# Gated linear attention in pairs of chunks: two chunks' products side by side, the state known two chunks ahead, and a start of its own

## The chip, the cores and the metric

The kernel runs on one core of one Trainium2 chip. A core has TensorE (matmuls and transposes), VectorE, ScalarE and GpSimd for elementwise work, and queues from which DMAs are issued; SyncE, ScalarE and GpSimd issue them here. The metric is the device time of one execution in microseconds (us), the median of several runs. The profile is that of one execution; its span (432.3 us) is a little shorter than the time of the run it was taken in (434.06 us).

## The reference, cut to what matters

Two stages follow one another. The first is a gated recurrence over 768 steps for 4 x 8 heads of 48 features; the second sends each of the 3072 resulting tokens through the one of 8 experts that its gate likes best.

```python
def _attn_ref(q, k, v, alpha):              # each (4, 8, 768, 48)
    for t in range(S):
        state = alpha[:, :, t, :, None] * state + einsum('bhd,bhe->bhde', k[:, :, t], v[:, :, t])
        y[:, :, t] = einsum('bhd,bhde->bhe', q[:, :, t], state)

def _moe_ref(x, w_gate, w1, w2):            # x (3072, 384), 8 experts, hidden 1024
    expert_idx = argmax(x @ w_gate, axis=1)
    # rows sorted by expert; for each expert e:
    #   y = relu(x_e @ w1[e]) @ w2[e]
    return gate_w[:, None] * y              # gate_w: softmax weight of the chosen expert
```

The kernel cuts each sequence into 6 chunks of 128 steps, 24 chunks in all (`s` = 0 to 23; `c = s % 6` is the place in the sequence). Within a chunk the recurrence is a masked product of matrices; between chunks only a state `U` of 48 x 48 per head is carried.

## The kernel before: the parts that the change touches

For one chunk the work is, by name: `logs` (ln of alpha), `cums` (running sum of the logs by a triangular matmul, then the two exponentials), `decay_out` and `decay_in` (the chunk's total decay goes through DRAM to be turned from a row into columns `E`), `operands` (k and q times the exponentials), `transposes`, `scores` (k times q, masked), `attend` (results from the state, from the scores, and the products for the next state), `rows` (back to tokens x features, with the gate logits), `keep_rows` (to DRAM). Every four chunks `choose` picks the experts, `rank_products` and `slots_of` count the ranks, `one_hots` prepare the table from which `tokens_of_slots` builds the gather lists.

```python
def transposes(s):
    for i, n in enumerate(("kT", "qT")):
        tp = ps.tile([C, NP, C], F32, name="tp", bufs=2)
        for p in range(NP):
            nc.tensor.transpose(tp[:, p, :], pair(kqb[s % 4][:, i], p), ident[:])
        ...                                  # qT copied by VectorE, kT by ScalarE

def scores(s):                               # 48-row operands, 128-column outputs
    for p in range(NP):
        for t, r in ((sA, 0), (sB, DP)):
            nc.tensor.matmul(t[:, p, :], lhsT=d["kT"][r : r + D, p, :], rhs=d["qT"][r : r + D, p, :], ...)
    # dA = sA * cmask on VectorE; dB = copy of sB on ScalarE, masked by GpSimd

def attend(s):
    ...
    if c > 0:                                # from the state: 48 rows, 64 columns
        for n in range(NP // 2):
            for p in (n, n + NP // 2):
                for a in range(2):
                    nc.tensor.matmul(yp(p)[...], lhsT=st[s - 1]["U"][r : r + D, p, :], rhs=d["qT"][r : r + D, p, :], ...)
    for p in range(NP):                      # from the scores: 128 rows, 64 columns
        for a in range(2):
            nc.tensor.matmul(yp(p)[...], lhsT=d["v"][:, 2 * p + a, :], rhs=d["d" + "AB"[a]][:, p, :], ...)
    if c + 1 < NB:                           # for the next state: 128 rows, 64 columns
        ... nc.tensor.matmul(kv[...], lhsT=kqb[s % 4][:, 0, 2 * p + i, :], rhs=d["v"][:, 2 * p + i, :D], ...)
    nc.vector.tensor_copy(d["yT"][:, : NP // 2, :], y[:])
    nc.vector.tensor_copy(d["yT"][:, NP // 2 :, :], y2)
    # U = (kv + U of s-1) * E : VectorE adds, GpSimd multiplies

for s in range(-4, NT - 1):                  # one chunk per turn
    loads(s + 5)
    do(attend, s)
    do(scores, s + 1)
    ...                                      # ranks, when a group of chunks is complete
    do(cums, s + 3)
    do(operands, s + 3)
    ...                                      # one_hots or slots_of
    do(transposes, s + 2)
    do(rows, s)
    do(keep_rows, s)
    do(decay_out, s + 3)
    do(decay_in, s + 2)
    do(logs, s + 4)
    late_consts(s)
    ...                                      # choose; some loads of expert 0's weights

s = NT - 1                                   # the end of the stage
attend(s)
...                                          # transposes of two blocks gathered early
while hots:
    one_hots(hots.pop(0))
tokens_of_slots(0, 9)
slots_of(*rank_products(groups_of[-2], ...)) # chunks 21 and 22
rows(s); keep_rows(s); choose(groups_of[-1]) # chunk 23
one_hots(hots.pop(0), nc.gpsimd); one_hots(hots.pop(0))
tokens_of_slots(9, NT - 3)
go_ahead(1)                                  # steps of expert 0's first layer on the early blocks
slots_of(*rank_products(groups_of[-1], ...))
go_ahead(4)
one_hots(hots.pop(0))
tokens_of_slots(NT - 3, NT)
slots(0); fetch_lot(1, ...)                  # the other gathers of expert 0
```

Every engine takes its instructions in the order in which this program names them. After the attention stage the experts follow, from about 160 us to the end; the change does not touch them.

Of the kernel before, what the change touches and what calls it, by code (L numbers as in the profile page):

```python
# [8 lines left out]
F32 = mybir.dt.float32  # L9
# [9 lines left out]
def kernel(  # L19
# [10 lines left out]
):  # L30

# [54 lines left out]
    ends = list(range(0, NT - 7, 4)) + [NT - 5, NT - 3, NT - 1, NT]  # L86
    groups_of = [range(a, b) for a, b in zip(ends, ends[1:])]
    ORD = NT - 5

    TE = ORD - ORD % 4  # L90
    EB = 2
    EC = EB * C
    assert EB * C <= TE * C < N and TE * C > N // 2 and EB * NQ <= NU
# [189 lines left out]
    with tc.tile_pool(name="ld", bufs=6) as ld, \  # L283
# [20 lines left out]
        def loads(s):  # L304
            load("k", s + 1)
            load("q", s + 1)
            load("a", s + 2)
            load("v", s)
# [11 lines left out]
        def cums(s):  # L320
            d = st[s]
            cum = rps.tile([C, Dm], F32, name="cum")
            nc.tensor.matmul(cum[:], lhsT=cmask[:], rhs=d["ln"][:], start=True, stop=True)  # L323
            d["icp"] = work.tile([C, Dm], F32, name="icp")
            d["cp"] = work.tile([C, Dm], F32, name="cp", bufs=3)
            nc.scalar.activation(d["icp"][:], cum[:], AF.Exp, scale=-1.0)  # L326
            nc.scalar.activation(d["cp"][:], cum[:], AF.Exp)
# [15 lines left out]
        def operands(s):  # L343
            d = st[s]
            kq = kqb[s % 4]
            nc.gpsimd.tensor_tensor(kq[:, 0, :, :D], d["k"][:], heads(d["icp"]), op=ALU.mult)  # L346
            nc.gpsimd.tensor_tensor(kq[:, 1, :, :D], d["q"][:], heads(d["cp"]), op=ALU.mult)  # L347

        def transposes(s):
            d = st[s]  # L350
            for i, n in enumerate(("kT", "qT")):
# [3 lines left out]
                d[n] = work.tile([C, NP, C], F32, name=n, bufs=3)  # L355
# [23 lines left out]
        def attend(s):  # L379

            d = st[s]
            c = s % NB

            y = ps.tile([C, NP // 2, C], F32, name="y")
            kvp = ps.tile([C, 2 * C + NP * D + 4 * E], F32, name="kvp")
            y2 = kvp[:, : 2 * C].rearrange("r (p t) -> r p t", p=NP // 2)
            kv = kvp[:, 2 * C : 2 * C + NP * D].rearrange("r (p d) -> r p d", p=NP)

            def yp(p):
                return y[:, p, :] if p < NP // 2 else y2[:, p - NP // 2, :]  # L390

            if c > 0:
                for n in range(NP // 2):
                    for p in (n, n + NP // 2):
                        for a in range(2):
                            r = a * DP
                            nc.tensor.matmul(  # L397
                                yp(p)[at(p, a) : at(p, a) + DP, :],
                                lhsT=st[s - 1]["U"][r : r + D, p, :], rhs=d["qT"][r : r + D, p, :],
                                start=(n == 0), stop=False, skip_group_check=True,  # L400
                            )
            for p in range(NP):
                for a in range(2):
                    nc.tensor.matmul(  # L404
                        yp(p)[at(p, a) : at(p, a) + DP, :], lhsT=d["v"][:, 2 * p + a, :], rhs=d["d" + "AB"[a]][:, p, :],
                        start=(c == 0 and p % (NP // 2) == 0), stop=True, skip_group_check=True,
                    )
            d["yT"] = work.tile([C, NP, C], F32, name="yT")
            d["ranks"] = kvp[:, 2 * C + NP * D :]
            if c + 1 < NB:  # L410
                for p in range(NP):
                    for i, r in enumerate((0, DP)):
                        nc.tensor.matmul(  # L413
                            kv[r : r + DP, p, :], lhsT=kqb[s % 4][:, 0, 2 * p + i, :], rhs=d["v"][:, 2 * p + i, :D],
                            start=False, stop=True, skip_group_check=True,
                        )
            nc.vector.tensor_copy(d["yT"][:, : NP // 2, :], y[:])
            nc.vector.tensor_copy(d["yT"][:, NP // 2 :, :], y2)
            if c + 1 < NB:
                d["U"] = Ub[s % len(Ub)]  # L420
                E_b = d["E"][:].unsqueeze(2).to_broadcast([C, NP, D])
                if c > 0:
                    acc = work.tile([C, NP, D], F32, name="acc")
                    nc.vector.tensor_tensor(acc[:], kv[:], st[s - 1]["U"][:, :, :D], op=ALU.add)
                    nc.gpsimd.tensor_tensor(d["U"][:, :, :D], acc[:], E_b, op=ALU.mult)
                else:
                    nc.vector.tensor_tensor(d["U"][:, :, :D], kv[:], E_b, op=ALU.mult)

        def rows(s):
# [3 lines left out]
            for p in range(NP):  # L433
                nc.tensor.matmul(xr[:, p, :], lhsT=d["yT"][:, p, :], rhs=back[:, p, :], start=True, stop=True)  # L434
# [32 lines left out]
        def slots_of(g, pos):  # L467
# [16 lines left out]
            if g[0] == ORD:  # L484
                turns(pos3[0:1, 0, :])
# [89 lines left out]
        for n in "akq":  # L575
            load(n, 0)
        load("a", 1)
        loads(0)
        first_consts()
        keep_busy(4)  # L580
        parts = fetch_parts(0)
        hots = []
        for s in range(-4, NT - 1):
# [368 lines left out]
```

## Time and profile before

| | |
|---|---|
| time, median of 3 | 434.94 us (434.81 to 436.13) |
| span of the profile | 432.3 us |
| PE busy | 422.4 us, 98% |
| DVE / ACT / POOL busy | 147.3 / 107.1 / 138.9 us |
| attention, first reading of a state (chunk 1) | 19.82 us |
| the same for chunk 23, the last | 143.88 us |
| last count of the ranks (PE, line 671) | 151.40 us |
| granted TensorE clock | 1.00 of full speed |

A line of the timeline gives start, length, engine, line of the kernel, operation and its tiles; a matmul's `48*64` is rows times columns of the array that it uses. In brackets stands how long the engine had been idle before it and what ended that. The ends of matmuls are modelled, so the distance between starts tells more than their lengths.

### The profile page before, as it was taken

How to read it: one execution, taken by the hardware profiler on the slowest of the kernel's cores; microseconds unless marked ns; L12 is line 12 of the kernel's file. 1: busy time of each engine (PE TensorE's matmuls, PEld its weight loads, DVE VectorE, ACT ScalarE, POOL GpSimd, SP SyncE). 2: the span in 40 equal slices, each digit the busy share in tenths (PEclk: the TensorE clock that was granted, in tenths of full speed). 3: DMA queues.
4: the chain of work that ended last, by engine and by line, in shares of the span. 5: the costliest groups of instructions: out<-in, count | busy, mean ns of one | idle time of the engine just before them, and what ended most of it. 6: DMA issues, size and time to landing. Idle time of an engine off the chain costs nothing.

```text
span 432.3 us, 7834 instructions
## 1 busy us (share of the span) xinstructions
PE 422.4 (98%) x2986; PEld 285.7 (66%) x2986; DVE 147.3 (34%) x454; ACT 107.1 (25%) x218; POOL 138.9 (32%) x247
## 2 busy tenths in 40 slices
PE   8999999999999999999999999999999999999995
PEld 5788888888878898555555555655655455555452
DVE  3546766766778833721012101201201101111100
ACT  4545554544453321110111111011110110011011
POOL 4667675656565450160160110025010010010011
PEclk9999999999999999999999999999999999999999
DMA  9999999999834741995531710624530050000000
GB/s 161 187 196 205 205 209 199 207 191 187 187 82 118 215 121 46 395 399 179 204 111 45 279 38 12 245 87 122 202 126 20 0 183 18 0 34 18 1 34 29
DMA packets 128434, 59.41 MB, mean 137 GB/s; under 512 B 110462, under 2 KB 123320, under 8 KB 128394
## 3 DMA queue, kind: packets, MB, share of 16 engines
q1 hardware_dynamic: 116258, 48.87, 45.2%
q0 software_dynamic: 3328, 9.94, 7.1%
q10 hardware_dynamic: 8808, 0.08, 1.2%
q8 instruction: 24, 0.39, 0.4%
q14 instruction: 16, 0.13, 0.1%
HBM read 49.30 MB, written 9.96 MB: 137 GB/s over the span
## 4 chain that ended last, share of the span: by engine, by line
PE 58%; issue 28%; DMA 4%; POOL 4%; SPq 2%; DVE 1%; ACT 0%; POOLq 0%; ACTq 0%; DVEq 0%
PE zp L806 16%; PE hp L790 14%; PE sA L367 4%; PE xr L434 4%; PE tp L354 4%; PE cum L323 3%; POOL out_dram L812 3%; PE y L404 3%; PE hp L653 3%; PE y L397 2%; DMA q_sb<-in_q_dram 2%; PE kvp L404 2%; PE kvp L413 2%; SPq L302 1%; PE xtp L782 1%
## 5 line engine op out<-in xcount | busy, mean ns | idle before, releaser
L806 PE MATMUL zp<-w,h_sb 128*128 128x384 f32 (+2 forms) x560 | 137.1, 487 | 0.0
L790 PE MATMUL hp<-xT,w 128*128 128x416 f32 (+3 forms) x384 | 125.1, 486 | 0.0
L806 PEld LDWEIGHTS zp<-w,h_sb 128*128 128x128 f32 (+2 forms) x560 | 73.6, 163 | 56.4 <-issue 14.8
L790 PEld LDWEIGHTS hp<-xT,w 128*128 128x128 f32 x384 | 71.7, 190 | 51.9 <-issue 37.8
L812 POOL DMA_INDIRECT out_dram<-zo,o_idx x26 | 25.8, 992 | 220.3 <-ACT zo L811 215.4
L795 DVE TENSOR_SCALAR h_sb<-hp 128x416 f32<-128x416 f32 (+3 forms) x32 | 17.9, 558 | 149.7 <-PE hp L790 149.7
L811 ACT ACTIVATE zo<-zp,gw 128x384 f32<-128x384 f32 x26 | 15.1, 580 | 123.7 <-PE zp L806 110.0
L797 ACT ACTIVATE h_sb<-hp 128x416 f32<-128x416 f32 (+3 forms) x32 | 15.7, 490 | 107.3 <-PE hp L790 107.3
L784 DVE COPY xT<-xtp 128x384 f32<-128x384 f32 (+3 forms) x29 | 12.9, 484 | 46.1 <-PE xtp L782 46.1
L367 PE MATMUL sA<-qT,kT 48*128 48x128 f32 x192 | 27.7, 284 | 0.6 <-DVE lgn L436 0.6
L265 POOL DMA_INDIRECT xg<-x_rows,g_idx x26 | 25.1, 965 | 9.7 <-issue 6.9
L367 PE MATMUL sB<-qT,kT 48*128 48x128 f32 x192 | 27.7, 285 | 0.0
L346 POOL TENSOR_TENSOR kqb<-k_sb,icp 128x384 f32<-128x384 f32 x24 | 24.4, 1015 | 9.5 <-ACT icp L326 7.2
L354 PEld LDWEIGHTS tp<-ident,kqb 128*128 128x128 f32 x192 | 22.4, 140 | 7.2 <-issue 4.2
L434 PE MATMUL xr<-back,yT 128*128 128x104 f32 x192 | 25.1, 273 | 0.0
L354 PE MATMUL tp<-ident,kqb 128*128 128x128 f32 x192 | 24.9, 273 | 0.0
L367 PEld LDWEIGHTS sA<-qT,kT 48*128 48x128 f32 x192 | 23.1, 187 | 2.6 <-issue 1.2
L323 PE MATMUL cum<-ln,cmask 128*128 128x384 f32 x48 | 22.1, 543 | 2.6 <-ACT ln L312 2.4
L347 POOL TENSOR_TENSOR kqb<-q_sb,cp 128x384 f32<-128x384 f32 x24 | 24.0, 1001 | 0.0
L434 PEld LDWEIGHTS xr<-back,yT 128*128 128x128 f32 x192 | 23.3, 192 | 0.1
L367 PEld LDWEIGHTS sB<-qT,kT 48*128 48x128 f32 x192 | 23.1, 187 | 0.0
L374 POOL TENSOR_SCALAR_AFFINE_SELECT dB<-dB 128x512 f32<-128x512 f32 x24 | 15.3, 636 | 22.2 <-ACT dB L373 19.8
(170 smaller groups left out, 475.6 us busy)
## 6 DMA issues: line engine op xcount, KB each, us to landing
w<-in_moe_w_dram SPq DMA_DIRECT2D x14, 1536.0 KB
x_rows<-xs SPq DMA_DIRECT2D x24, 196.0 KB
a_sb<-in_alpha_dram SPq DMA_DIRECT2D x24, 192.0 KB
k_sb<-in_k_dram SPq DMA_DIRECT2D x24, 192.0 KB
q_sb<-in_q_dram SPq DMA_DIRECT2D x24, 192.0 KB
vb<-in_v_dram SPq DMA_DIRECT2D x24, 192.0 KB
w<-in_moe_w_dram SPq DMA_DIRECT2D x12, 128.0 KB
w<-in_moe_w_dram SPq DMA_DIRECT2D x8, 192.0 KB
```

Of the source, the lines that this page charges most:

```text
L265: nc.gpsimd.indirect_dma_start(out=xg[:, j, :], out_offset=None, in_=x_d[: N + 1 if n else TE * C + 1, :], in_offset=bass.IndirectOffsetOn ...
L323: nc.tensor.matmul(cum[:], lhsT=cmask[:], rhs=d["ln"][:], start=True, stop=True)
L346: nc.gpsimd.tensor_tensor(kq[:, 0, :, :D], d["k"][:], heads(d["icp"]), op=ALU.mult)
L347: nc.gpsimd.tensor_tensor(kq[:, 1, :, :D], d["q"][:], heads(d["cp"]), op=ALU.mult)
L354: nc.tensor.transpose(tp[:, p, :], pair(kqb[s % 4][:, i], p), ident[:])
L367: nc.tensor.matmul(t[:, p, :], lhsT=d["kT"][r : r + D, p, :], rhs=d["qT"][r : r + D, p, :], start=True, stop=True,)
L404: nc.tensor.matmul(yp(p)[at(p, a) : at(p, a) + DP, :], lhsT=d["v"][:, 2 * p + a, :], rhs=d["d" + "AB"[a]][:, p, :], start=(c == 0 and p % ...
L434: nc.tensor.matmul(xr[:, p, :], lhsT=d["yT"][:, p, :], rhs=back[:, p, :], start=True, stop=True)
L790: nc.tensor.matmul(hp[:, c0:c1], lhsT=w1[:, a, f * C : (f + 1) * C], rhs=xT[:, a, c0:c1], start=(a == 0), stop=(a == DB - 1),)
L795: nc.vector.tensor_relu(h[:, f, c0:c1], hp[:, c0:c1])
L806: nc.tensor.matmul(zp[i * wd : (i + 1) * wd, :], lhsT=h[:, f, c : c + wd], rhs=w2[:, f, :], start=(f == 0), stop=(f == FB - 1), skip_group ...
L812: ins = nc.gpsimd.indirect_dma_start(out=out[:, :], out_offset=bass.IndirectOffsetOnAxis(ap=idx, axis=0), in_=zo[:], in_offset=None, bound ...
```

## The change

Two chunks are worked on in one turn. The results of both from the state are made one after the other, then the products for the next two states, then the four groups of results from the scores, so that matmuls that use the same shape of the array stand side by side. The two states that the next pair reads are finished a whole turn ahead. The two chunks' results share PSUM banks and are copied out in two large copies instead of four. The products for the states go to the banks of the scores; ScalarE copies those of the even chunks. Logs, sums and operands run five and six chunks ahead. The first pair, and all that runs ahead of the first full turn, has a hand-written order; chunk 0's operands are made by VectorE. The groups of chunks for the choice of experts become 4, 4, 4, 4, 4, 2, 2 instead of 4, 4, 4, 4, 3, 2, 2, 1, and the end of the stage handles the last pair at once.

The core of the diff (cuts marked):

```diff
-    ends = list(range(0, NT - 7, 4)) + [NT - 5, NT - 3, NT - 1, NT]
+    ends = list(range(0, NT - 3, 4)) + [NT - 2, NT]
...
-        for n in "akq":
-            load(n, 0)
-        load("a", 1)
-        loads(0)
+        some_loads("a0 k0 q0 a1 k1 q1")
         first_consts()
         keep_busy(4)
+        back_consts()
+        logs(0)
+        cums(0)
+        keep_busy(3)
+        operands(0, nc.vector)
+        ...
+        transposes(2)
+        cums(3)
+        operands(3)
+        logs(4)
+        decay_out(2)
+        decay_in(2)
+        some_loads("a6 v3 v4")
+        rows(0)
+        keep_rows(0)
+        state(1)
+        cums(4)
+        operands(4)
+        decay_out(3)
+        decay_in(3)
+        some_loads("k5 q5 a7")
+        rows(1)
+        keep_rows(1)
+        products(2)
+        logs(5)
+        scores(2)
+        decay_out(4)
+        state(2)
+        some_loads("k6 q6 a8 k7 q7")
+        cums(5)
+        transposes(3)
+        logs(6)
+        operands(5)
+        decay_in(4)
+        ...
+        cums(6)
+        transposes(4)
+        ...
+        scores(3)
+        operands(6)
+        ...
-        for s in range(-4, NT - 1):
+        for s in range(2, NT - 2, 2):
+            loads(s + 8)
+            y = results_of(s)
+            reads(s)
+            reads(s + 1)
+            products(s + 1)
+            products(s + 2)
+            weighs(s, 0)
+            weighs(s + 1, 0)
+            results_to(s, y, 0)
+            weighs(s, 1)
+            weighs(s + 1, 1)
+            results_to(s, y, 1)
+            state(s + 1)
+            state(s + 2)
+            do(logs, s + 5)
+            scores(s + 2)
+            do(logs, s + 6)
+            do(cums, s + 5)
+            transposes(s + 3)
+            do(operands, s + 5)
+            rows(s)
+            keep_rows(s)
+            do(cums, s + 6)
+            ...                              # ranks, counts, early slots
+            do(transposes, s + 4)
+            do(decay_out, s + 5)
+            do(decay_in, s + 4)
+            loads(s + 9)
+            rows(s + 1)
+            keep_rows(s + 1)
+            do(operands, s + 6)
+            scores(s + 3)
+            do(decay_out, s + 6)
+            do(decay_in, s + 5)
+            late_consts(s)
+            late_consts(s + 1)
             for r in ranked:
                 slots_of(*r)
+            if s == TE:
+                close_early(counts[0:1, 0:1])
+            if s == ORD:
+                turns(counts[0:1, :])
+            for _ in range(min(2, len(hots))):
+                one_hots(hots.pop(0))
+            if s == TE + 4:
+                fetch_lot(0)
             for g in groups_of:
-                if g[-1] == s:
+                if g[-1] == s + 1:
                     choose(g)
...
-        s = NT - 1
+        s = NT - 2
-        attend(s)
+        y = results_of(s)
+        reads(s)
+        reads(s + 1)
+        ranks = ps.tile([C, NP, C], F32, name="sA")[:, 0, :]
+        r = rank_products(groups_of[-2], ranks[:, : len(groups_of[-2]) * E])
+        weighs(s, 0)
+        weighs(s + 1, 0)
+        results_to(s, y, 0)
+        weighs(s, 1)
+        weighs(s + 1, 1)
+        results_to(s, y, 1)
         ...                                  # transposes of the early blocks
+        rows(s)
+        keep_rows(s)
+        tokens_of_slots(0, NT - 8)
+        rows(s + 1)
+        keep_rows(s + 1)
+        choose(groups_of[-1])
         while hots:
             one_hots(hots.pop(0))
-        tokens_of_slots(0, 9)
-        slots_of(*rank_products(groups_of[-2], st[s]["ranks"][:, : len(groups_of[-2]) * E]))
-        rows(s)
-        keep_rows(s)
-        choose(groups_of[-1])
+        slots_of(*r)
         one_hots(hots.pop(0), nc.gpsimd)
         one_hots(hots.pop(0))
-        tokens_of_slots(9, NT - 3)
+        tokens_of_slots(NT - 8, NT - 4)
...
-        slots_of(*rank_products(groups_of[-1], mps.tile([C, Dm], F32, name="zp")[:, :E]))
-        go_ahead(4)
+        slots_of(*rank_products(groups_of[-1], mps.tile([C, Dm], F32, name="zp")[:, : 2 * E]))
+        tokens_of_slots(NT - 4, NT - 2)
+        go_ahead(6)
+        one_hots(hots.pop(0), nc.gpsimd)
         one_hots(hots.pop(0))
-        tokens_of_slots(NT - 3, NT)
+        tokens_of_slots(NT - 2, NT)
```

In the new turn, `reads` is the part of `attend` that reads the state, `weighs(s, h)` one half of the results from the scores, `products` and `state` the two halves of the state's update, and `results_to` the copy of the results of both chunks.

## Prediction

> **What bounds the kernel now.** I first read busy time by stage, to see which engine ends the attention stage.
>
> ```profile
> 20.00:30.00 10.00, 10.00 (x153) 8.58 (x150) 4.62 (x11) 4.78 (x10) 6.04 (x14) 1.00 0.99 178
> 60.00:80.00 20.00, 20.00 (x297) 17.24 (x287) 14.57 (x39) 9.80 (x21) 12.75 (x31) 1.00 1.09 207
> 100.00:120.00 20.00, 18.71 (x266) 16.18 (x260) 14.37 (x38) 9.78 (x21) 10.53 (x24) 1.00 0.88 178
> ```
>
> The columns are window, length, then busy time of PE, weight load, DVE, ACT, POOL, granted clock, DMA share, GB/s. From 20 us on PE has no gap to speak of, and DVE, the next, has a quarter of its time free. So the stage costs what PE's instructions cost, and a gain must come from there. Next, PE's timeline for one chunk, with the starts:
>
> ```profile
> 65.49 0.33 PE L397 MATMUL y<-qT,Ub 48*64 48x128 f32 x2
> ...
> 66.09 0.32 PE L404 MATMUL y<-dA,vb 128*64 128x128 f32 x1
> ...
> 67.01 0.62 PE L413 MATMUL kvp<-vb,kqb 128*64 128x48 f32 x16
> 67.56 0.37 PE L367 MATMUL sA<-qT,kT 48*128 48x128 f32 x1
> ...
> 68.44 0.27 PE L367 MATMUL sA<-qT,kT 48*128 48x128 f32 x1
> ...
> 68.65 0.91 PE L323 MATMUL cum<-ln,cmask 128*128 128x384 f32 x2
> 69.40 1.04 PE L354 MATMUL tp<-ident,kqb 128*128 128x128 f32 x8
> 70.28 1.04 PE L434 MATMUL xr<-back,yT 128*128 128x104 f32 x8
> 71.24 0.33 PE L397 MATMUL y<-qT,Ub 48*64 48x128 f32 x2
> ```
>
> One chunk takes 71.24 - 65.49 = 5.75 us. By starts: state reads 0.60, results from scores 0.92, state products 0.55, scores 1.09, sums 0.75, transposes 0.88, rows 0.96. Within one shape a step lasts 0.11 us (four reads, two score products, or one transpose matmul); at that pace reads would take 0.44, results 0.88, scores 0.88, rows 0.88. The excess, 0.16 + 0.04 + 0.21 + 0.08 = 0.49 us, sits at the four places where the shape changes (48x64, 128x64, 48x128, 128x128): 0.12 us each.
>
> Then ACT, because the new start leans on it:
>
> ```profile
> 60.07 0.48 ACT L441 COPY xs<-xr 128x384 f32<-128x384 f32 x1 [0.60 <-POOL kqb L346]
> 60.15 0.24 ACTq L331 DMA_DIRECT2D decay_rows<-cp  x1
> 60.48 0.80 ACTq L339 DMA_DIRECT2D Eb<-decay_rows  x2
> 61.33 0.52 ACT L312 ACTIVATE ln<-a_sb 128x384 f32<-128x384 f32 x1 [0.78 <-DMA decay_rows<-cp]
> ```
>
> The two decay reads cost ACT's queue 0.80 us although the row they read went out a chunk earlier: the row of 60.15 is for the chunk after. Last, the end of the stage on PE, which has hardly a gap:
>
> ```profile
> 146.78 1.12 PE L434 MATMUL xr<-back,yT 128*128 128x104 f32 x8
> 147.74 0.86 PE L535 MATMUL cum<-oh_c,oh_r 128*128 128x128 f16 x12
> 148.83 0.70 PE L653 MATMUL hp<-xT,w 128*128 128x256 f32 x2 [0.23 <-ACT xs L441]
> 149.36 0.17 PE L463 MATMUL zp<-ohs,ones_sq 128*128 128x8 f16 x1
> 149.39 0.17 PE L464 MATMUL zp<-oh,lt_strict 128*128 128x8 f16 x1
> 149.42 1.97 PE L653 MATMUL hp<-xT,w 128*128 128x256 f32 x8
> ```
>
> Expert steps (L653) fill the time in which DVE counts ranks.
>
> [...] The trace has no landing times for the small decay rows; it does show the DMA engines fully loaded here (share 0.99 to 1.09). [...] clock 1.00 throughout.
>
> **Part 1, the full turns: a gain.** A pair had eight shape changes; in the new turn it has five (reads to products, results to scores, scores to sums, rows to scores, scores to reads). Three times 0.12 is 0.37 us: 11.13 instead of 11.50 us a pair. I walked one turn through the built program's order with the durations of this trace. Nothing on DVE, ACT or POOL is late; the tightest is the mask of the second chunk's scores (POOL, about 0.5 us early). From 29.5 us (explained below) to the first read of chunk 22, the kernel before needs 112.1 us. The ten new turns need 10 x 11.13, less 3 x 0.44 (no state at a sequence's first chunk), 3 x 0.55 (no product at its last), 3.1 (one sum from turn 18, two sums and a transpose from turn 20: 0.75 + 1.50 + 0.88), plus 1.0 for ranks and early lists: 106.2. Gain 5.9 us: 3.7 are shape changes, the rest small stalls of before (the idle 1.3 us near 116 us is one), which I assume gone.
>
> **Part 2, the start: a loss.** At the first full turn the new program has done all that the old one has at 25.58 us (first read of chunk 2), plus two sums (1.5), one transpose (0.88), one scores (1.0) and one product (0.55): the old kernel's equal point is 29.5. New, from the program order: chunk 0's operands on DVE, an estimated 0.55 us each (between its 192-element add at 0.35 and its 512-element copy at 0.69), instead of POOL's 1.0, bring scores 0 from 10.8 to about 9.3. By rows 0 (about 21.2, before 21.9) PE still leads by 0.7. Then ACT takes over: logs 4, decay out 2, decay in 2, copy of rows 0, exponentials 4, decay out 3, decay in 3, copy of rows 1, copy of product 2, logs 5. Each decay in reads the row that the instruction just ahead of it sent, so ACT stands still for the trip[...]. In numbers: decay out 2 ends 21.5, decay in 23.0 to 23.9, copy of rows 0 to 24.4, exponentials to 25.2, decay in 3 at 26.5 to 27.3, copy of rows 1 to 27.8, copy of product 2 to 28.0, logs 5 to 28.5, logs 6 (after scores 2, sums 5, exponentials 5 and kT 3) to 31.9. PE waits for them: rows 1 needs the one bank that the copy of rows 0 frees (1.9 us), scores 2 the bank of product 2 (2.1 us), sums 6 the logs 6 (1.1 us). The first full turn begins at about 34.7: loss 5.2 us.
>
> **Part 3, the end: the larger loss.** Let T be the first read of chunk 22. The last full turn puts on DVE, behind the mask of scores 23: ranks of four chunks and the order of experts (12 small operations; the like took 138.39 to 140.78, 2.4 us), two one-hots (143.52 to 144.75, 1.2 us), the choice for chunks 20 and 21 (five operations, 1.0 us). That is T + 5.3, and POOL's sums T + 5.9. On PE their ranks stand before the results from the scores. PE does its reads (1.0 us) and waits 4.9 us. Then results to T + 7.9, early transposes, rows 22 after the second large copy to 9.4, sixteen list products (0.058 each) to 10.3, rows 23 to 11.3. The next list products need one-hots that stand on DVE behind the choice for 22 and 23: to 13.9, PE idle 2.5. One expert step (0.44), ranks, then lists that need GpSimd's one-hot (1.4 us, as at 149.45): 16.5, idle 2.0. Six steps (2.6 us), lists, last count at T + 19.35. The old kernel from its equal point (143.88 less reads, results and rows of one chunk, 2.3: 141.6) to its last count at 151.40 needs 9.8, with five steps done, not seven. The two more are worth 0.9. Loss 19.35 - 9.8 - 0.9 = 8.65 us.
>
> **Sum.** -5.9 + 5.2 + 8.65 = +8.0 us, so 442.9. The experts after that are as before and PE-bound, so nothing gives it back. I shade it to 442.5, because the start was written by hand, perhaps against shorter trips than mine.
>
> **Rivals.**
> - *The turns win and the ends cost little.* For it: PE is the bound for 120 us, and the mode changes are real. It needs the decay trip near nothing (start 2 to 3 us better) and DVE finished earlier than its own order allows. Against: twenty-odd DVE operations after scores 23 cannot hide behind 1 us of reads. Time 430 to 434.
> - *ACT or POOL becomes the bound in the turns.* POOL gains an addition; ACT has copies, logs, exponentials and decays, some 9.5 of 11.1 us when queue time is counted. Against: their deadlines are half a turn away. If masks came late each turn by 0.5 us: 447.
> - *The clock.* [...] half speed for the next 3 us or more would add 2 to 3 us: 445.
> - *DMA hides or sets the start.* Loads land about 0.95 us apart (chunk 1's alpha by 7.55, the ninth load by 12.0), so the 20th, alpha 6, is there at about 22, before the logs 6 of my chain. Loads do not bound it.
>
> **Range and chances.** Uncertain: the start by 2 us[...], the end by 1.5, the turns by 2 (stalls gone or new), the clock by up to 3 upwards. Together some 3.5 us, with more room below for a part seen too darkly: 435.5 to 448. Two per cent is 8.7 us, or 443.6, just above my value: slower by over 2% 0.38, within 0.60, faster by over 2% 0.02.
>
> **What would show it.** Reads of neighbouring pairs 11.1 us apart (wrong: 11.5 or more); the first read of chunk 2 near 34.7, with ACT's gaps ahead of the decay reads of chunks 2 and 3 (wrong if near 30); PE idle about 5 us between the reads of chunk 23 and the ranks, and about 2 us twice after (wrong if those ranks start within 2 us); and the clock in that stretch. It is wrong as a whole if DVE has done the choice before the reads end, or the decay row is back within 0.5 us.

## The result, and the profile after

The changed kernel takes 454.54 us (median; 453.81 to 456.66), the kernel before, beside it on the same chip, 434.88 us. The ratio is 1.0453, with a 95% interval of 1.0414 to 1.0493: slower by 4.5%. The profiled execution spans 452.8 us against 432.3, so 20.5 us are to be explained. The prediction had 442.5 us, 435.5 to 448: the direction was right, but the time lies outside the range.

In the views PE is TensorE, DVE VectorE, ACT ScalarE, POOL GpSimd and SP SyncE. First the same view as before the change, busy time by stage (window, length, busy time of PE, weight load, DVE, ACT, POOL, then granted clock, DMA share, GB/s), of the changed kernel, with one stretch of its end added:

```profile
20.00:30.00 10.00, 7.39 (x56) 5.77 (x55) 1.97 (x5) 4.54 (x11) 4.63 (x7) 0.84 0.96 186
100.00:120.00 20.00, 18.98 (x288) 16.54 (x286) 11.82 (x33) 10.18 (x23) 12.22 (x27) 1.00 0.88 174
150.00:160.00 10.00, 5.72 (x48) 5.36 (x44) 5.01 (x22) 0.78 (x2) 3.04 (x5) 0.66 0.84 263
```

PE now idles 2.6 us of ten in the start, where it had no gap before, and 4.3 us of ten in the end; in both the clock is below 1. In this stretch of the turns it idles 1.0 us of twenty, which is no more than before (1.3). What PE waited for, in total (us, times, longest), from the view of waits:

```profile
PE sA L498 <- POOL ohs L493: 4.3, 1, 4.3
PE cum L498 <- ACT cp L337: 4.1, 4, 1.0
...
PE cum L568 <- DVE oh_c L561: 1.9, 2, 1.7
```

The first and the last line are the end and were predicted. The second, four waits of 1.02 us ahead of the rank products, was not. From 36 to 149 us, the turns, PE waits besides them only 0.5 us for masks and 0.5 us for a copy. Three marks in PE's timeline divide the stage as the prediction did: the first read of chunk 2, the first read of chunk 22 (T) and the last count. For the kernel before, the first two are its equal points.

| us | before | predicted | after |
|---|---|---|---|
| first read of chunk 2 | 29.5 | 34.7 | 36.15 |
| from there to T | 112.1 | 106.2 | 112.84 |
| from T to the last count | 9.8 | 19.35 | 22.61 |
| from the last count to the end | 280.9 | 280.0 | 281.2 |

In the start, ACT's timeline (its DMA issues are `ACTq`; in brackets the idle time before, and what ended it):

```profile
21.26 0.24 ACTq L343 DMA_DIRECT2D decay_rows<-cp  x1
...
22.88 0.81 ACTq L351 DMA_DIRECT2D Eb<-decay_rows  x2
23.73 0.48 ACT L476 COPY xs<-xr 128x384 f32<-128x384 f32 x1 [1.38 <-DMA decay_rows<-cp]
...
26.76 0.48 ACT L476 COPY xs<-xr 128x384 f32<-128x384 f32 x1 [1.78 <-DMA decay_rows<-cp]
```

The decay row is out at 21.50 and read at 22.88: a trip of 1.38 us. The prediction's chain has 1.5 there (21.5 to 23.0), the author's assumption, which no trace of the kernel before shows. ACT stands for the trip twice, as foreseen. Then the clock falls (this view is of PE alone: window, length, PE busy, clock, DMA share, GB/s):

```profile
26.00:28.00 2.00, 0.90 (x6) 0.70 1.04 195
28.00:30.00 2.00, 2.00 (x15) 0.50 1.16 241
```

It stays at 0.50 to 32 us and is 0.60 from 32 to 34.

In the turns, a turn that has rank products, from PE's timeline:

```profile
79.33 0.19 PE L498 MATMUL cum<-ohs,ones_sq 128*128 128x32 f16 x1 [1.02 <-ACT cp L337]
```

The ranks are written into the spare columns of the PSUM tile whose sums ACT is just reading for its two exponentials (78.40 to 79.27), and stand on PE ahead of transposes that do not need those exponentials. The two-chunk periods from 36.15 on are 11.06, 11.94, 10.87, 12.34, 10.89, 12.28, 11.05, 11.97, 10.43, 10.01; the four near 12 are the four whose ranks share that tile. The end, on PE:

```profile
148.99 1.10 PE L409 MATMUL y<-qT,Ub 48*64 48x128 f32 x32
154.38 0.17 PE L498 MATMUL sA<-ohs,ones_sq 128*128 128x16 f16 x1 [4.28 <-POOL ohs L493]
...
164.55 0.22 PE L568 MATMUL cum<-oh_c,oh_r 128*128 128x128 f16 x1 [1.66 <-DVE oh_c L561]
...
167.40 0.37 PE L568 MATMUL cum<-oh_c,oh_r 128*128 128x128 f16 x2 [1.56 <-POOL oh_c L561]
167.56 4.09 PE L794 MATMUL hp<-xT,w 128*128 128x256 f32 x12
...
171.60 0.17 PE L814 MATMUL cum<-ohs,ones_sq 128*128 128x8 f16 x1
```

All three waits of the prediction are there, each a little shorter than predicted (4.9, 2.5, 2.0). But what lies between them is slower: from 154.38 to the early transposes at 158.12 3.7 us, at a clock of 0.50, for work that takes 2.02 at 1.00 (154.41 to 156.43 in the run with TensorE kept busy, below), and six expert steps 3.9 us (167.56 to 171.49, with 0.50 from 168 to 170) instead of 2.64 at 1.00 (155.43 to 158.07 in the run with the new end, below). The prediction had 1.9 and 2.6.

### The profile page after: what moved, and what is told of

The parts are those of the page before. It is cut to its first block, busy times and chain, and to the rows that moved or that the text cites. A ratio compares the mean times of both kernels' runs of the same rounds, so it can differ in the third digit from the quotient of the medians.

```text
span 452.8 us, 7737 instructions
## 1 busy us (share of the span) xinstructions
PE 427.7 (94%) x2981; PEld 288.9 (64%) x2981; DVE 134.9 (30%) x408; ACT 108.7 (24%) x230; POOL 144.6 (32%) x259
## 3 DMA queue, kind: packets, MB, share of 16 engines
q0 software_dynamic: 3328, 9.94, 6.7%
## 4 chain that ended last, share of the span: by engine, by line
PE 61%; issue 27%; POOL 4%; DVE 3%; ACT 2%; DMA 1%; ACTq 0%; POOLq 0%
PE zp L949 15%; PE hp L933 13%; PE sA L379 5%; PE y L421 5%; PE tp L366 4%; PE xr L469 4%; PE cum L331 3%; POOL out_dram L955 3%; PE hp L794 3%; PE y L409 2%; PE sB L443 1%; PE xtp L925 1%; PE xr L597 1%; PE sA L443 1%; POOL xg L267 1%
## 5 line engine op out<-in xcount | busy, mean ns | idle before, releaser
L379 PE MATMUL sA<-qT,kT 48*128 48x128 f32 x192 | 28.7, 290 | 1.2 <-DVE qT L369 1.1
L369 DVE COPY qT<-tp 128x512 f32<-128x512 f32 x24 | 16.6, 691 | 35.0 <-PE tp L366 35.0
L927 DVE COPY xT<-xtp 128x384 f32<-128x384 f32 (+3 forms) x29 | 13.0, 484 | 46.8 <-PE xtp L925 46.1
L358 POOL TENSOR_TENSOR kqb<-k_sb,icp 128x384 f32<-128x384 f32 x23 | 23.0, 1001 | 11.0 <-ACT icp L336 10.9
L366 PE MATMUL tp<-ident,kqb 128*128 128x128 f32 x192 | 26.1, 280 | 0.0
L421 PE MATMUL y<-dA,vb 128*64 128x128 f32 x192 | 25.4, 286 | 0.0
L421 PE MATMUL y<-dB,vb 128*64 128x128 f32 x192 | 25.0, 287 | 0.0
```

Of the source, the lines that this page charges most:

```text
L358: eng.tensor_tensor(kq[:, 0, :, :D], d["k"][:], heads(d["icp"]), op=ALU.mult)
L369: nc.vector.tensor_copy(d[n][:], tp[:])
L421: nc.tensor.matmul(d["y"][h][at(p, a) : at(p, a) + DP, n, :], lhsT=d["v"][:, 2 * p + a, :], rhs=d["d" + "AB"[a]][:, p, :], start=False, st ...
```

## Experiments

In each, times are medians of the executions; "before" is the kernel before, run beside it. Positions are from the profiled execution.

### One suspected cost at a time

**Ranks late.** In the turns of chunks 2 to 16 the rank products move behind the second chunk's rows, where ACT has long read the sums.

```diff
-            ranked = [rank_products(...) for g in groups_of if g[-1] == s - 1]
-            ...
             do(transposes, s + 4)
             ...
             rows(s + 1)
             keep_rows(s + 1)
+            ranked = [rank_products(...) for g in groups_of if g[-1] == s - 1]
```

> The only edit: in the full turns up to that of chunk 18, the rank products stand after the rows of the second chunk instead of right behind the sums whose PSUM tile they share. Theory (the rank products wait for the exponentials that read the same tile): the four turns with ranks, which took 11.9 to 12.3 us, take 10.6 to 11.2 like their neighbours, no wait of 1.0 us is left ahead of them, and the time falls by 4.0 to 5.5 us against the changed kernel. Rival (ACT is what those turns wait for, and the wait only moves to the next instruction): less than 1.5 us.

Measured: 451.41 us (ratio 1.0363, 1.0329 to 1.0397), 3.1 us less than the changed kernel, where 4.0 to 5.5 were expected. The waits of 1.02 us are gone: in PE's timeline rows start at 78.63, the ranks at 79.51, the next scores at 79.64. The turn from 69.64, with ranks, takes 11.09. But the turns as a whole only went from 112.84 to 111.56, because two early ones became longer: 12.69 from 44.95 and 12.00 from 57.64. There PE now waits 1.23 and 0.65 us for a copy of ACT (`accB`, at 50.42 and 62.46). This run also began its turns at 33.90 instead of 36.15, with the same program up to there, at full clock (the same view as above):

```profile
26.00:28.00 2.00, 1.35 (x19) 1.00 1.04 185
28.00:30.00 2.00, 2.00 (x15) 1.00 1.25 241
```

Of the 2.25 us, 0.30 were there before the clock fell (a sum at 22.10 instead of 22.40), so about 1.95 go with the half clock. The start at full clock is 0.8 us better than the prediction's 34.7. The edit doesn't touch the start, so that part of the gain is not its doing: between the two profiles (2.3 us apart) the turns are 1.28 us shorter, and the stretch from T to the last count is 1.1 us longer.

**Decay reads later in the start.** The reads of chunks 2 and 3 each move behind the next chunk's write, so that no read directly follows its own write.

```diff
         decay_out(2)
-        decay_in(2)
         ...
         decay_out(3)
-        decay_in(3)
+        decay_in(2)
         ...
         decay_out(4)
+        decay_in(3)
```

> The only edit: at the start, the decay reads of chunks 2 and 3 stand behind the next chunk's decay write instead of right behind their own. Theory (ACT stands still for the trip to DRAM, and PE waits for ACT): ACT's waits of 1.4 and 1.8 us go, the first read of chunk 2 comes at 31.5 to 33 us instead of 36.15, the clock stays at 1.00 through the start, and the time falls by 3 to 4.5 us. Rival (loads bound the start, or later loads take the gain back): first read at 35 or later, time within 1 us.

Measured: 455.36 us (1.0468, 1.0438 to 1.0497), first read of chunk 2 at 35.17. ACT no longer stands at the trips of chunks 2 and 3, and PE's waits at 24.26 and 27.52 shrink to one of 0.27 us. A new one takes their place: 2.62 us at 30.98, for the logarithm of chunk 6, which stands on ACT behind the read of chunk 3's decay and the exponentials held up with it; then the clock is at 0.60 and 0.54 from 30 to 34. The first read came 1 us earlier instead of 3 or more, and the time did not fall.

**Ranks of chunks 20 and 21 behind the last results**, which need none of them.

```diff
-        ranks = ps.tile([C, NP, C], F32, name="sA")[:, 0, :]
-        r = rank_products(groups_of[-2], ...)
         weighs(s, 0)
         ...
         results_to(s, y, 1)
+        ranks = ps.tile([C, NP, C], F32, name="sA")[:, 0, :]
+        r = rank_products(groups_of[-2], ...)
```

> The only edit: at the end, the rank products of chunks 20 and 21 stand behind the results of the last pair instead of ahead of them. Theory (PE waits at those ranks for DVE's queue): PE does the results at once, and the wait moves to the rows of chunk 22, whose copies DVE still makes behind the choice; last count minus first read of chunk 22 falls from 22.6 to 17 to 19 us, time lower by 4 to 6 us. Rival (the half clock of that stretch costs the time, and any wait as long brings it about): falls by less than 2 us.

Measured: 455.72 us (1.0474, 1.0433 to 1.0516); the last count at T + 23.85, later than before the edit. PE's timeline shows what took the place of the 4.28 us:

```profile
154.10 0.17 PE L498 MATMUL sA<-ohs,ones_sq 128*128 128x16 f16 x1 [2.32 <-POOL ohs L493]
...
155.70 0.90 PE L773 MATMUL tp<-ident,xg 128*128 128x128 f32 x3 [1.41 <-DMA xg<-x_rows,g_idx]
```

The results move ahead. PE still waits for the same choice, then 1.41 us (and another 0.86 at 157.46) for the landing of the early gather, which GpSimd issues behind its mask of the last scores (in the changed kernel, where it stands in the same place, at 150.66 and 152.17); the clock is at 0.63 from 154 to 158 and at 0.52 to 162.

**TensorE kept busy in that wait**, with eight products of zeros ahead of the ranks.

```diff
+        keep_busy(8)
         ranks = ps.tile([C, NP, C], F32, name="sA")[:, 0, :]
```

> The only edit: eight dummy products of 256 columns (about 3.9 us) fill the wait ahead of the ranks of chunks 20 and 21; no wait is taken away. Theory (the idle 4.3 us let the clock fall to half, and that costs time of its own): the clock from 152 to 160 us stays at 1.00, the results and early transposes take half the time, last count minus first read of chunk 22 falls from 22.6 to 19.5 to 20.5, time lower by 2 to 3.5 us. Rival (only DVE's order counts there, the clock is a sign without a cost): less than 0.7 us.

Measured: 455.26 us (1.0486, 1.0429 to 1.0543). The clock is 1.00 from 150 to 166, yet the last count comes at T + 21.92, only 0.7 us earlier: now PE waits 1.33 us for the same gather at 158.30, then 1.66 and 1.56 for the one-hots as before, and the clock falls to 0.57 from 166 to 170 after those. So half clock in the end is a loss, but here most of it fills time in which PE would otherwise wait.

**Reads taken apart.** A full turn gets two more changes of array shape. The edit also puts the first products sooner behind the scores whose bank they take.

```diff
             reads(s)
-            reads(s + 1)
             products(s + 1)
+            reads(s + 1)
             products(s + 2)
```

> The first full turns' order of reads and products is undone in part: reads of a chunk, products, reads of the next chunk, products; two changes of array shape more per turn, everything else as in the changed kernel. If a change of shape costs TensorE 0.12 us, as the prediction took from the kernel before, a turn without other waits grows from 11.05 to 11.3-11.4 us and the time from 454.5 to 457-458. If what the shapes cost is not in the changes, or the turns are paced by something else, less than 1 us is seen: 454-455.5.

Measured: 459.29 us (1.0559, 1.0522 to 1.0596), 4.75 us more than the changed kernel, more than expected. The same stretch of an undisturbed turn, first in the changed kernel, then in this one, on PE:

```profile
105.53 1.10 PE L409 MATMUL y<-qT,Ub 48*64 48x128 f32 x32
...
107.53 0.29 PE L421 MATMUL y<-dA,vb 128*64 128x128 f32 x1
```

```profile
108.61 0.67 PE L409 MATMUL y<-qT,Ub 48*64 48x128 f32 x16
109.46 0.67 PE L443 MATMUL sA<-vb,kqb 128*64 128x48 f32 x16 [0.18 <-DVE dA L383]
...
111.16 0.29 PE L421 MATMUL y<-dA,vb 128*64 128x128 f32 x1
```

From the first read to the first result, 2.00 us become 2.55. Of the 0.55, 0.18 is a wait for the bank that DVE's mask is still reading; 0.37 remains for two changes, 0.18 each, rather more than the 0.12 of the prediction. Fewer changes of shape are so worth having. But the 4.75 us are not all theirs: PE's waits for the mask rise from 0.5 to 3.0 us in all (seven, the longest 0.78), and the turns at the ends of sequences get one more change or none, eleven in all, or 2.0 us at 0.18.

### Why early turns stall: loads, or the issue of small transfers

**Fewer loads**, with late ranks. The `q` of chunks 2 to 9 is not loaded and `k` stands in its place: 1.57 MB are left out, and the rows of those chunks are not the attention asked for.

```diff
-            if s >= NT:
+            if s >= NT or (n == "q" and 2 <= s < 10):
                 return
             ...                       # operands: k where q is not loaded
```

> The kernel with the rank products moved late, and the q of chunks 2 to 9 not loaded (k stands in its place): 8 x 196 KB, 1.57 MB, are left out, 7.7 us of the DMA engines at the 203 GB/s that they moved. Theory that the loads pace the changed kernel's first turns, since two chunks more of a, k and q must have landed: the turns from 44.95 and 57.64 us, which took 12.69 and 12.00, take 11.1 to 11.4, the first read of chunk 8 comes at 66.5-67.5 instead of 69.64, the time falls from 451.4 to 448.5-449.5. Rival, that the decay's trips or the engines' order pace them whatever the loads: first read of chunk 8 at 69 or later, time 450.5-452.

Measured: first reads at 32.89, 43.95, 54.64, 65.51: the turns of 12.69 and 12.00 us take 10.69 and 10.87, and chunk 8 is read 4.1 us earlier. T is 141.92 instead of 145.46. The time is 446.83 us (1.0276, 1.0246 to 1.0305), 4.6 us less, more than the 2 to 3 expected. Loads have to do with the stalls.

**The same for the kernel before.**

> The kernel before, with the q of chunks 2 to 9 not loaded (k stands in its place), the same 1.57 MB left out. If only the changed kernel is paced by the loads in its first turns, the kernel before gains at most what its start waits for until 20 us: time 432.5-435, its turns stay at 11.5 us. If loads pace both, it gains as much as the changed kernel does, 2 to 3 us: 432 or less.

Measured: first read of chunk 2 at 25.59 (before: 25.58), that of a later chunk at 122.19 (122.56), last count at 151.03 (151.40): the loads do not pace its attention. The time, 467.87 us (1.0781, 1.0737 to 1.0825), where 432.5 to 435 was expected, says nothing of them: from the last count on it takes 313.6 us instead of 280.9. The changed rows send tokens to other experts, and here the program for extra blocks runs: its 24 list products (`oh_xr`) stand at 426.8 to 436.5, and from 400 to 460 us PE is busy for only 46.1. They are in neither trace of the kernel before and after, nor in the run above, which takes 281.3 us from its last count on. Only the attention is read from this run.

### A new end

**Choice and gather ahead of the last scores**, with late ranks. The order of experts is computed after the last slots, the ranks of 20 and 21 stand behind the last results, half of the last results' copy goes to ScalarE, one of GpSimd's one-hots goes to VectorE, and list products and early transposes fill the gaps.

```diff
+            if s == ORD:
+                fetch_lot(0)
             rows(s + 1)
             keep_rows(s + 1)
+            if s == ORD:
+                choose(groups_of[-2])
             ...
-                turns(counts[0:1, :])
+                nc.vector.tensor_copy(first[:], counts[0:1, :])   # turns(first) after slots(0)
```

> The kernel with the rank products moved late, and the end in a new order: the choice of chunks 20 and 21 and the early gather ahead of the last scores, the turns of the experts after the slots, the rank products behind the last results, tokens of earlier chunks and early transposes as filling. Theory that the order on VectorE and GpSimd makes the end long and the half clock only follows from the idle TensorE: the last count comes 11 to 12.5 us after the first read of chunk 22 instead of 23.7, no stretch of 4 us after it at a clock under 0.8, time 438.5-442 instead of 451.4. Rival, that another wait takes the place of each one removed, as in the three runs on the end and start so far: last count 17 us or more after that read, time 445 or more.

Measured: 440.90 us (1.0137, 1.0104 to 1.0170), 10.5 less than with late ranks alone. The end, on PE:

```profile
145.54 1.10 PE L409 MATMUL y<-qT,Ub 48*64 48x128 f32 x32
148.69 0.18 PE L498 MATMUL sA<-ohs,ones_sq 128*128 128x16 f16 x1
...
158.19 0.17 PE L830 MATMUL cum<-ohs,ones_sq 128*128 128x8 f16 x1
```

The ranks wait for nothing, the longest wait up to the last count is 0.93 us (rows 23, for ACT's copy of rows 22), the next 0.57 (expert steps, for ACT's early copies), the clock is 1.00 throughout, and the last count comes at T + 12.65. So the three waits, the late gather and the half clock go together, with the order on VectorE and GpSimd; neither of the two single repairs above had shortened the end by more than 0.7 us. Two operations also changed their engine, and how much each part of the edit brings was not taken apart.

### The stand at the decay transfers

In the run with the new end the early turns still stall (13.30 us from 44.75, 11.84 from 58.05). ACT's timeline there:

```profile
44.73 0.48 ACT L476 COPY xs<-xr 128x384 f32<-128x384 f32 x1 [1.31 <-DMA q_sb<-in_q_dram]
45.11 0.59 ACT L385 COPY dB<-sB 128x512 f32<-128x512 f32 x1
47.76 0.24 ACTq L343 DMA_DIRECT2D decay_rows<-cp  x1
48.30 2.06 ACTq L351 DMA_DIRECT2D Eb<-decay_rows  x2
50.46 0.32 ACT L451 COPY accB<-sB 128x192 f32<-128x192 f32 x1 [4.76 <-DMA Eb<-decay_rows]
```

In the last line ACT has nothing to do but issue three small transfers, and stands 4.76 us; PE then waits 2.12 us for the copy that stands behind them. The row to be sent was computed by 43. The first line is a sign of what holds the issues: a copy of rows, which has no use for `q`, starts late behind two decay reads, and the wait is put down to a load of `q`. What each issue stands for, no view shows. Ahead of the write at 47.76, SyncE issued a load of `q` (42.86), a load of `v` (44.34) and a row store (45.49); that ACT stood for one of these older transfers was the author's estimate, which no run shows.

**The same transfers on SyncE's queue**, from chunk 6 on; in the run above that queue's issues already waited for other engines, up to 1.4 us, between 43 and 60 us. Loads and needs are unchanged.

```diff
-                nc.scalar.dma_start(e_d[s : s + 1, :], st[s]["cp"][C - 1 : C, :])
+                (nc.sync if s >= 6 else nc.scalar).dma_start(e_d[s : s + 1, :], st[s]["cp"][C - 1 : C, :])
...                                    # decay_in the same
```

> The kernel with the new end (440.9 us); from chunk 6 on, the small decay transfers are issued by SyncE, which issues the loads, instead of by ScalarE. Loads, arithmetic and needs are the same. Theory that the first turns stall because ScalarE stands at the issue of a decay transfer until an older load has landed[...], not because data are missing: the two turns of 13.30 and 11.84 us (from 44.75 and 58.05) fall to 11.0-11.5 each, the first read of chunk 22 comes at 142-143.5 instead of 145.54, time 437.5-439.5. Rival, that the turns wait for the data of the loads themselves: those turns stay above 11.8, time within 1 us of 440.9.

Measured: 438.97 us (1.0097, 1.0075 to 1.0119). The two turns take 10.71 and 10.86, T is 143.47. In the same place ACT now goes on at once:

```profile
45.08 0.59 ACT L385 COPY dB<-sB 128x512 f32<-128x512 f32 x1 [0.42 <-PE sB L379]
46.75 0.32 ACT L451 COPY accB<-sB 128x192 f32<-128x192 f32 x1 [1.08 <-PE sB L443]
```

The rival that the data of the loads were missing is out for these two turns: all loads are still made, and the stalls are gone. Why fewer loads helped as well was not shown.

**All decay transfers from chunk 2 on SyncE's queue**: the same edit with `s >= 2`.

> As the run beside it, but the decay transfers of chunks 2 to 4 in the start too are issued by SyncE. If ScalarE's stand at those issues is what makes TensorE wait in the start (0.56, 1.23, 0.47 and 1.04 us), the first read of chunk 2 comes at 31.5-33 instead of 33.70 and the time falls by another 0.5-2 us, to 436-438.5. If SyncE comes to them later than ScalarE did[...], the state of chunk 2 is late and the first read comes at 34 or later.

Measured: 443.11 us (1.0188, 1.0162 to 1.0213). The first read of chunk 2 comes at 32.27, as the first theory had it: ACT's stand does hold up the start. But now the loads stand behind the decay in SyncE's queue (DMA share 0.69 from 26 to 34 us, where the two runs above have 1.26 and 1.29), and the turns from 32.27 on took 13.15, 12.59 and 14.42 us. In the first of them PE waits 1.67 us for a mask that GpSimd makes late; in the second 1.17 us for a load of `v`; in the third 1.81 us for a copy by ACT. In the start either ACT's work or the loads wait.

**The last two waits of the end, and chunk 4's decay.** A PSUM tile of their own for the last rows, the early copies first, and `s >= 4`.

```diff
+            if s == NT - 1:
+                xr = ps.tile([C, NP, C], F32, name="sB")[:, :, : D2 + E]
         rows(s + 1)
-        keep_rows(s + 1)
         ...                       # early transposes and their copies
+        keep_rows(s + 1)
```

> The fastest so far (438.97 us) with two small steps: the last rows get a PSUM tile of their own and the early transposes' copies go ahead of the last rows' copy (TensorE waited 0.93 and 0.57 there), and SyncE issues the decay transfers from chunk 4 on instead of 6 (TensorE waited 1.05 for a logarithm behind chunk 4's). If waits on the path are worth their length: last count 11 to 11.6 us after the first read of chunk 22 instead of 12.65, first read of chunk 2 at 32.8-33.3 instead of 33.89, time 436-437.5. If the next obstacle takes them: 438 or more. Neither brings it below the kernel before, 434.4.

Measured: 437.98 us, before 435.83 beside it (1.0052, 1.0035 to 1.0069); 436 to 437.5 was expected. The last count comes at T + 11.41, as expected. The first read of chunk 2 comes at 36.08, not 33: in this profile the start fell to half clock again (0.57 from 26 to 34), so the step for chunk 4 can't be read. T is 143.74 all the same, since the turns took 107.66 instead of 109.58.

**The queue alone**, on the changed kernel.

> The changed kernel with one thing altered: SyncE issues the decay transfers from chunk 6 on. With the ranks late the first turns' stalls at these issues cost about 2 us (13.30 and 11.84 fell to 10.71 and 10.86 in the new-end kernel, 1.9 us in the time). In the changed kernel itself the ranks' waits and a late start hide most of it: first read of chunk 22 at 147-148.7 instead of 148.99, time 452.5-454.5 instead of 454.5. If the issue waits were the main loss of its turns, 451 or less.

Measured: 453.36 us (1.0406, 1.0378 to 1.0434), 1.2 us less than the changed kernel, with intervals that overlap. T is 148.09 instead of 148.99, but that comes from the start (first read of chunk 2 at 35.36): the turns take 112.73 us, against 112.84. In the changed kernel itself the stand costs PE next to nothing; it comes to light only when the waits of the ranks are gone.

The steps together:

| | first read of 2 | to T | T to last count | time, us |
|---|---|---|---|---|
| changed kernel | 36.15 | 112.84 | 22.61 | 454.54 |
| ranks late | 33.90 | 111.56 | 23.71 | 451.41 |
| and new end | 33.70 | 111.84 | 12.65 | 440.90 |
| and decay on SyncE | 33.89 | 109.58 | 12.65 | 438.97 |
| and last two waits | 36.08 | 107.66 | 11.41 | 437.98 |
| before (equal points) | 29.5 | 112.1 | 9.8 | 434.1 to 435.8 |

The best of them is still slower than the kernel before, by 0.5%: in its profile the pairs bring 4.4 us in the turns, and the start (6.6 us) and the end (1.6 us) take more. In the profiles at full clock where ScalarE still issues the start's decay transfers, the start took 4.2 to 4.4 us. No run here beats the kernel before.

## Why the prediction was wrong

**The sum.** Predicted -5.9 (turns), +5.2 (start), +8.65 (end): +8.0. Measured +0.7, +6.65 and, as 22.61 - 9.8 + 0.3, +13.1: +20.5. The directions held for the two ends; the gain in the turns was not there. Of the 12.5 us between the sums, the turns make 6.6, the end 4.5 and the start 1.45.

**The turns.** The step that failed is "Nothing on DVE, ACT or POOL is late". The estimate of the full turn itself was good: two without ranks lasted 11.06 and 11.05 us, predicted 11.13, and reads apart confirmed what pays, though a change of shape was put at 0.12 us and measured 0.18 there. What the walk missed in the changed kernel is ACT's exponentials: the ranks share a PSUM tile with the sums that these read, and PE waits four times 1.02 us for them, 4.1 of the 6.6 us; shown by moving the ranks. That alone brought 1.28 us in the turns, for behind it lay a second thing that the walk missed: ACT stands at the issue of decay transfers, which is shown by moving the issue. That it stands there for unrelated transfers was not shown; the one sign of it is the trace's line at 44.73, 1.31 us put down to a load of `q`. The kernel before already had that sign, in its view of waits:

```profile
ACT ln L312 <- DMA q_sb<-in_q_dram: 1.7, 2, 0.9
```

A logarithm has no use for `q`. The prediction counted ACT's queue time, but held its deadlines to be half a turn away. With both taken away the turns took 107.66 us in one run and 109.58 in another; the 1.5 to 3.4 us above 106.2 were not taken apart in full. Part of it stands in the last two turns (10.52 and 10.01 us, where the prediction's terms give 9.94 and 8.75 before the 1.0 us for ranks and lists). The idle 1.3 us that the prediction places near 116 in the kernel before end at 118.1 and 120.0; nothing rests on the place.

**The start.** The mechanism was as predicted: the trip took 1.38 us (1.5 assumed), ACT stood 1.38 and 1.78 us, and PE waited for rows 1, scores 2 and sums 6, though less than written (0.94, 1.10 and 0.24 us against 1.9, 2.1 and 1.1; at full clock 1.36, 0.65 and 1.04). At full clock that came to 33.90, against 34.7. The term left out is the clock: at about half speed from some 27 to 33 us it cost about 1.95 us. The prediction had the clock as a rival for the end alone. That ACT's stand at the decay trip holds the start was only half of the matter, as later reads and all reads on SyncE showed: each removed the stand and met the next obstacle, the logarithm of chunk 6 or the loads.

**The end.** The order was read rightly: DVE's choice was done at T + 5.05 (predicted 5.3), POOL's sums at T + 5.6 (5.9), PE waited 4.28 (4.9). The mis-sized terms are those after: results and transposes at half clock (3.7 us to the transposes instead of 1.9, and 1.34 for them instead of 0.66), the six expert steps 3.9 instead of 2.6, together 3.8 us, less 1.9 for waits shorter than predicted; the other 1.4 us above T + 19.35 were not taken apart. That is what the rival *the clock* had said, with its "2 to 3 us". That half clock follows such a wait was an assumption there, for in the trace of the kernel before the clock is 1.00 throughout; in the trace after, the wait of 4.28 us is followed by a clock of 0.50 from 154 to 158. So it belonged in the sum. Yet the clock alone was not the cure: kept up, it left T + 21.92. "The two more are worth 0.9" failed too. The 16 expert steps after the last count and the transposes behind them stay where they are. What shrinks is the rest of that group of expert steps (6 matmul records before, 2 now), and PE then waits 0.55 us for an activation, where it had no wait before: from the last count to the next group of matmuls it takes 8.97 us before, 8.82 after.

**The rivals.** *The turns win and the ends cost little* was out from the first profile. *ACT or POOL becomes the bound* came true in a form not thought of: ACT had time, but PE waited for its exponentials through a shared tile and, once these were out of the way, for a copy behind a transfer. *DMA hides or sets the start*: no wait of PE or of a logarithm in the changed kernel is put down to a load, as the prediction argued; in the later runs transfers acted mostly through the issue of others. The range was too narrow above: the uncertainties were added as independent errors of size, while in the end a waiting PE was followed by half clock, so that a late step also made the steps behind it longer.

## What to carry to other kernels

When work is moved, walk not only its inputs but all that its instruction waits for: the PSUM tile that someone else is reading (four waits of 1.02 us here), and what stands ahead of it on its engine, issues of transfers among it (ACT stood 4.76 us there). Here it paid to take small transfers off the queue of an engine whose arithmetic is on the path, where another queue had time for them: 1.9 us gained from chunk 6 on, 4.1 us lost when those of the start moved too. The end's waits, which came from late engines, were mended by their order (11.1 us less from T to the last count), not one by one (0.7 us at most); and an estimate in which TensorE waits must carry the clock as a term, for 4.28 us of waiting were followed here by 0.50.

## What was not expected of the hardware

- Half clock came after waits far below the 4.28 us of the end. In the changed kernel PE waited 0.56, 0.94 and 1.10 us between 21.8 and 27.5, and the clock was at 0.50 from 28 to 32. With late ranks it waited 0.56, 1.36 and 0.65 us in the same stretch and kept full clock. In the queue-alone run 0.56, 0.88 and 0.45 were followed by 0.50 from 28 to 30. What decides was not found; it is not the longest wait, nor their sum. Nor is it the program: six of the kernels here have the same one up to some 36 us, and from 28 to 30 us four of their profiles show 0.50 (changed kernel, ranks behind the last results, kept busy, reads apart), two 1.00 (ranks late, new end).
- A start at half clock (first read of chunk 2 at 36.08) and one at full clock (33.89) reached T within 0.3 us of each other, 143.74 and 143.47. The time came back from about 100 us on (turns of 11.05, 10.71 and 10.52 us against 11.31, 11.48 and 11.40). In the run with the early start PE waits there 0.42 and 0.41 us, at 113.36 and 125.17, for GpSimd's mask. In the other run PE has neither wait. What made the masks late in the run that was ahead was not shown. A gain in the start is not always a gain at T.
